# Batch 0's first transform stage on four 64x64 tiles, its input in pieces of 48 rows, its table and small inputs issued by ScalarE

## The chip, the cores and the metric

The kernel runs on one core of one Trainium2 chip. The metric is the device time of one execution in microseconds (us). The kernel before takes 1416.41 us, the median of three runs (1415.95 to 1417.36).

The engines are TensorE (PE for matmuls, PEld for weight loads), VectorE (DVE), ScalarE (ACT), GpSimd (POOL) and SyncE (SP), which here only issues DMAs. DMAs are issued in order on the queue of the engine that issues them.

## The reference

Two stages in float32. The first is a spectral layer on 4 batches of 3008 x 256, the second a mixture-of-experts style block with a rational activation on the 12032 resulting rows.

```python
X = np.fft.rfft(x, axis=1); Xr, Xi = X.real, X.imag
Yr = Xr @ w_r - Xi @ w_i + b_r
Yi = Xr @ w_i + Xi @ w_r + b_i
Yr, Yi = (np.sign(Y) * np.maximum(np.abs(Y) - 0.01, 0) for Y in (Yr, Yi))
y = np.fft.irfft(Yr + 1j * Yi, n=3008, axis=1).reshape(12032, 256)
h = y @ w_in                                    # 256 -> 2048
P = a[0] + a[1]*h + a[2]*h**2 + a[3]*h**3
Q = 1 + abs(b[0])*abs(h) + abs(b[1])*h**2
out = (P / (Q + 1e-6)) @ w_out                  # 2048 -> 256
```

## The kernel before

The transform of length 3008 = 64 x 47 is done as matmuls with tables. For each batch, stage f1 transforms along the 47 axis (rows padded to 48), its result goes out to a DRAM buffer `s1` and comes back with the axes turned (`b_all` for batch 0, `bt` for others); stage f2 transforms along the 64 axis; `m_task` mixes with w_r and w_i; `i1_task` is the first inverse stage, which goes out to `s2` and comes back as `ct`; `i2_task` is the last inverse stage and yields the input of the block, whose 208 units (L460, L553) are the main loop.

Batch 0's transform stands ahead of the main loop and is called the prologue here. It has these parts, in program order:

- Nine filler matmuls on a zero tile (`warm(9)`, L627), and eight loads of batch 0's input `x` on SP (`load_x`, L152). A load c holds four of the 32 columns j. Loads 0 and 1 have 96 rows of 4 KB, loads 2 to 7 have 128 rows, of which 96 are used.
- Stage f1 of batch 0 (`f1_first`, L173): 16 calls, two for each load c. A call is one float32 matmul of 96 rows by 128 columns of table `f1o` (a table with the two halves g interleaved) on 512 columns, then one copy out of PSUM, by ACT for the first call of a pair (L159) and by DVE for the second (L157). After a pair, SP stores 96 rows of 4 KB to `s1` (L187). Small steps that prepare bias and selection tiles (`prepare_small`) stand on DVE behind calls 9, 11, 13 and 15.
- On SP behind the stores: the first 8 of 24 pieces of table f2, the weights `wt`, the loads of `b_all` (L697, they need every store of `s1`), the rest of the tables, and the 16 raw loads of w_in and w_out, which come as float64 (L674).
- 33 filler matmuls (`warm(WARM)`, L729), then a loop over p of 12 pairs of frequencies: f2 (L255), mixing (L351, L358), i1 (L376). Between these stand the steps of the conversion of the raw weights to pairs of float32 tiles (`from_f64`, L597 to L611): five steps for each of 16 raw tiles, 80 in all. The numbers in `HC` and `HM` say how many steps stand at which p, `HF` how many behind the first five tasks of batch 1's stage f1.
- Batch 1's stage f1 (`f1_task`, L195), which runs on four tiles of 64x64: rows 0 to 47 and 64 to 111 hold the two halves g of the input, and each half is multiplied twice, for two pairs of columns.

All instructions stand on each engine in the order in which the program writes them. A DMA takes one of eight semaphores in turn (named DMAHW0 to DMAHW7 in the order), over both issuing engines, and an issue whose semaphore is still held by an earlier DMA waits for that one's landing.

Of the kernel before, what the change touches and what calls it, by code (L numbers as in the profile page):

```python
# [9 lines left out]
F32 = mybir.dt.float32  # L10
# [16 lines left out]
UB = NFC // FU  # L27
LAM = 0.01
WARM = 33
HC = (0, 0, 3, 3, 3, 3, 3, 3, 3, 3, 3, 3)  # L30
HM = (0, 0, 3, 4, 3, 4, 3, 4, 3, 4, 3, 4, 8, 0)
HF = (2, 3, 2, 0, 0)
I2Q = (5, 6)
SIZES = (5,) * 14 + (4,) + (5,) * 10 + (4,)
C0 = float(np.float32(1.0) + np.float32(1e-6))
# [2 lines left out]
def dft_tables():  # L38
    n2 = np.arange(N2)
    k2 = np.arange(NK)  # L40
    n1 = np.arange(N1)
    k1 = np.arange(N1)
    w = 2.0 * np.pi / N2
    ang = w * ((n2[:, None] * k2[None, :]) % N2)
    f1 = np.zeros((ROWS, NK, 2))
    f1[:N2, :, 0] = np.cos(ang)
    f1[:N2, :, 1] = -np.sin(ang)
    i2b = np.zeros((NK, NG, 2, NG, N2))
    i2 = np.zeros((NK, 2, N2))
# [24 lines left out]
    f1o = np.zeros((NG, ROWS, NK, 2, NG))
    for q in range(NG):
        f1o[q, :, :, :, q] = f1
    f1o = np.pad(f1o.reshape(96, 96), ((0, 0), (0, 32)))
# [12 lines left out]
    return {  # L90
        "f1": f1p.astype(f),
        "f1o": f1o.astype(f),
        "i2": i2p.astype(f),
        "f2": f2.reshape(128, NK * 128).astype(f),
        "g1": g.reshape(128, NK, 2, NG, NJ).swapaxes(2, 3).reshape(128, NK * 128).astype(f),
        "sel": sel.astype(f),
        "minus": -np.eye(128, dtype=f),
    }
# [3 lines left out]
def spectral_moe(ctx, tc, t, out):  # L102
# [39 lines left out]
    def load_x(b, c):  # L142
        if b == 1 and c in (2, 3):
            xt = pro3.tile([128, 4, D], F32, tag=f"x{c}", name="xin", bufs=1)
        elif b == 1 and c >= 6:
            xt = pro3.tile([128, 6, D], F32, tag=f"b{c - 6}", name="xin", bufs=1)[:, :4]
        elif b == 0 and c >= 2:
            xt = const.tile([128, 4, D], F32, tag=f"win{c}", name="xin")
        else:
            xt = sm.tile([128, 4, D], F32, tag="xin", name="xin")  # L150
        rows = 96 if b == 0 and c < 2 else 128
        nc.sync.dma_start(out=xt[:rows], in_=(t["x"][b - 1, c] if b else t["x0"][c])[:rows])  # L152
        xin[b, c] = xt

    def copy(eng, out, in_):
# [9 lines left out]
        while late:  # L165
            late.pop(0)()

    a_t = {}

    def new_s1(b):  # L170
        s1[b] = dram.tile([NK, 2, NG, NJ, D], F32, tag="s1", name="s1")

    def f1_first(i):  # L173
        c, r = divmod(i, 2)
        if i == 0:
            new_s1(0)
        pt = bank(0, "f1" if r else "")
        nc.tensor.matmul(out=pt, lhsT=f1o, rhs=xin[0, c][:96, 2 * r:2 * r + 2, :].rearrange("p j d -> p (j d)"),  # L178
                         start=True, stop=True)
        if not r:  # L180
            a_t[0] = const.tile([128, 4, D], F32, tag=f"wsp{c}", name="a")[:96]
        copy(r, a_t[0][:, 2 * r:2 * r + 2].rearrange("p j d -> p (j d)"), pt[:96])
        if r:
            del xin[0, c]
        if r or i >= 14:
            z = slice(2 * r, 2 * r + 2) if i >= 14 else slice(0, 4)
            nc.sync.dma_start(out=s1[0].rearrange("k c g j d -> (k c g) j d")[:, 4 * c + z.start:4 * c + z.stop, :], in_=a_t[0][:, z])  # L187

    def f1_task(b, c, pos):
        if pos == 0:  # L190
            new_s1(b)
        pts = [bank(b, "f1" if g else "m" if 4 <= pos < 6 else "") for g in range(NG)]
        for g, h in ((0, 0), (1, 1), (0, 1), (1, 0)):
            r = slice(64 * g, 64 * g + 48)
            nc.tensor.matmul(out=pts[g][64 * h:64 * h + 64], lhsT=f1[r],  # L195
                             rhs=xin[b, c][r, 2 * h:2 * h + 2, :].rearrange("p j d -> p (j d)"), start=True, stop=True)
# [415 lines left out]

    with tc.manual_schedule():
        nc.vector.memset(cb, 1.0)
        f1o = pro.tile([96, 128], F32, tag="f1o", name="f1o", bufs=1)
        nc.scalar.dma_start(out=f1o, in_=t["f1o"])
        nc.scalar.activation(out=cb, in_=cb, func=ACTF.Abs_reciprocal_sqrt)
        b_all = [pro3.tile([128, 6, D], F32, tag=f"b{z}", name="b_all", bufs=1) for z in range(4)]
        nc.vector.memset(offset, 0.0)
# [13 lines left out]
        eye = pro.tile([128, 128], F32, tag="eye", name="eye", bufs=1)  # L633

        def load_small():
            nc.sync.dma_start(out=sel, in_=t["sel"])
            for k, nm in enumerate(("b_r", "b_i")):
                nc.sync.dma_start(out=bsb[2 * k:2 * k + 2, :],
                                  in_=t[nm].rearrange("(o d) -> o d", o=1).to_broadcast([2, D]))
            nc.sync.dma_start(out=eye, in_=t["minus"])  # L640

        def prepare_small():
            nc.vector.memset(v32(selr), 0.0)
# [55 lines left out]
        def load_f2(a, z):  # L699
            nc.sync.dma_start(out=f2[:, a:z], in_=f2_src[:, a:z])  # L700
# [10 lines left out]

        load_small()
        small_steps = prepare_small()
        for i in range(16):
            f1_first(i)
            if i in (9, 11, 13, 15):
                next(small_steps, None)
        load_f2(0, 8)
        load_wt()
        prepare_mix()  # L720
        load_all(0, 2)
        load_all(2, 2)
# [8 lines left out]
        for p in range(np_ + 3):  # L731
# [11 lines left out]
            if p == 0:  # L743
                more_raw(2)
            elif p == 1:
                load_all(12, 6)
            elif p == 2:
                load_f2(12, 24)
                nc.sync.dma_start(out=ca, in_=t["a"].rearrange("(o d) -> o d", o=1).to_broadcast([128, 4]))
                nc.sync.dma_start(out=cb, in_=t["b"].rearrange("(o d) -> o d", o=1).to_broadcast([128, 2]))  # L750
                nc.sync.dma_start(out=i2, in_=t["i2"])
                nc.sync.dma_start(out=f1, in_=t["f1"])
            if p >= 1:
                more_raw(2)
            if p == 3:
# [188 lines left out]
```

## Time and profile before

| | us |
|---|---|
| median of three runs | 1416.41 |
| the profiled execution's own time | 1419.05 |
| its span, first to last instruction | 1417.3 |
| fillers and stage f1 of batch 0 end on PE | 21.7 |
| first matmul of f2 | 29.65 |
| first matmul of the main loop | 102.66 |

Times in the rows are counted from the span's start. The columns of the timeline are start, duration, engine, line, operation, output <- inputs, count of merged instructions, and in brackets the idle time before and what ended it. A float32 matmul shows as two records. The DMA share is the mean share of the 16 DMA engines' time that their packets took; where packets overlap it passes 100%.

### The profile page before, as it was taken

The page shows a single profiled execution, that of the slowest core. Times are in us where ns is not written, and L with a number is a line of the kernel's source. Part 1 is how long each engine was busy: PE and PEld are TensorE (multiplying, and loading weights), DVE is VectorE, ACT ScalarE, POOL GpSimd, SP SyncE. Part 2 cuts the span into 40 slices and gives each one's busy share as a digit, 9 for nine tenths or more (in the row PEclk, how much of TensorE's full clock was granted, in tenths as well). Part 3 has the DMA queues.
Part 4 walks back from the last instruction along what each step waited for, and adds up shares of the span by engine and source line. Part 5 has one row for each costly group of instructions (what it writes and reads, how often), then busy time and mean ns, then how long its engine had stood idle before and what let it go on. Part 6 is the DMA issues. An engine that isn't in the chain of part 4 may idle for free.

```text
span 1417.3 us, 20378 instructions
## 1 busy us (share of the span) xinstructions
PE 1390.0 (98%) x7279; PEld 1210.9 (85%) x7279; DVE 1291.5 (91%) x1304; ACT 1144.5 (81%) x1513; POOL 670.5 (47%) x444
## 2 busy tenths in 40 slices
PE   9998999999999999999999999999999999999997
PEld 4977889998878989898888899998888888888887
DVE  3779899898999989999989999999999999999998
ACT  2768887887888778888888778888888898888985
POOL 0444444444554444454545444444545555555553
PEclk9999999999999999999999999999999999999999
DMA  9966556556776556556687465656555465555543
GB/s 309 379 215 162 117 121 150 110 114 158 160 204 151 116 130 141 117 121 156 148 208 158 98 142 126 127 115 133 108 127 118 97 122 96 112 118 99 117 77 80
DMA packets 95657, 200.48 MB, mean 141 GB/s; under 512 B 10748, under 2 KB 51748, under 8 KB 95556
## 3 DMA queue, kind: packets, MB, share of 16 engines
q0 software_dynamic: 29664, 97.62, 38.0%
q1 hardware_dynamic: 65780, 101.51, 23.2%
q8 instruction: 58, 0.95, 0.3%
q14 instruction: 43, 0.35, 0.1%
q10 hardware_dynamic: 112, 0.05, 0.0%
HBM read 54.61 MB, written 37.49 MB: 65 GB/s over the span
## 4 chain that ended last, share of the span: by engine, by line
PE 72%; DVE 10%; issue 9%; ACT 5%; DMA 4%; SPq 0%; DVEq 0%; ACTq 0%
PE h L460 28%; PE acc L553 27%; PE pi L426 4%; PE pft L315 4%; DVE t L511 3%; DVE v L523 3%; PE pft L376 2%; DMA v<-s 2%; PE pft L297 2%; PE pft L255 2%; PE pft L195 1%; PE pft L178 1%; DVE g L520 1%; ACT t L499 1%; DMA s<-zt 1%
## 5 line engine op out<-in xcount | busy, mean ns | idle before, releaser
L553 PE MATMUL acc<-g,wsp 128*128 128x470 f32 (+1 forms) x2496 | 563.7, 375 | 3.4 <-DVE g L533 3.4
L527 POOL TENSOR_TENSOR t<-t,v 128x940 f32<-128x940 f32 (+1 forms) x206 | 469.7, 2280 | 164.4 <-DVE v L523 143.8
L553 PEld LDWEIGHTS acc<-g,wsp 128*128 128x128 f32 x2496 | 470.0, 190 | 62.8 <-DVE g L533 5.0
L460 PE MATMUL h<-xsh,win 128*128 128x470 f32 (+1 forms) x1664 | 436.9, 384 | 6.0 <-DVE t L512 5.6
L497 POOL DMA_DIRECT2D v<-s x206 | 181.6, 882 | 489.7 <-issue 452.9
L460 PEld LDWEIGHTS h<-xsh,win 128*128 128x128 f32 x1664 | 304.8, 189 | 61.6 <-PE acc L553 9.8
L520 DVE SCALAR_TENSOR_TENSOR g<-t,small,y 128x940 fp32r<-128x940 f32 (+1 forms) x208 | 250.3, 1203 | 45.8 <-ACT y L506 42.6
L492 ACT ACTIVATE v<-h 128x940 f32<-128x940 f32 (+1 forms) x208 | 196.2, 943 | 95.4 <-PE h L460 92.1
L511 DVE TENSOR_TENSOR t<-t,h 128x940 f32<-128x940 f32 (+1 forms) x208 | 231.3, 1112 | 27.3 <-ACT t L499 25.6
L512 DVE SCALAR_TENSOR_TENSOR t<-t,small,h 128x940 f32<-128x940 f32 (+1 forms) x208 | 245.2, 1179 | 7.4
L533 DVE SCALAR_TENSOR_TENSOR g<-t,small,y 128x940 fp32r<-128x940 f32 (+1 forms) x208 | 244.2, 1174 | 0.1
L460 PE MATMUL h<-xsl,win 128*128 128x470 f32 (+1 forms) x832 | 241.4, 371 | 0.0
L523 DVE SCALAR_TENSOR_TENSOR v<-v,g 128x940 f32<-128x940 f32 (+1 forms) x208 | 231.8, 1114 | 0.1
L504 ACT ACTIVATE y<-v 128x940 f32<-128x940 f32 (+1 forms) x208 | 206.1, 991 | 21.4 <-DMA v<-s 21.4
L499 ACT ACTIVATE t<-h,small 128x940 f32<-128x940 f32 (+1 forms) x208 | 216.2, 1039 | 0.0
L506 ACT ACTIVATE y<-y 128x940 f32<-128x940 f32 (+1 forms) x208 | 205.1, 986 | 2.0
L493 ACT ACTIVATE s<-h 128x940 f32<-128x940 f32 (+1 forms) x208 | 195.7, 941 | 0.0
L460 PEld LDWEIGHTS h<-xsl,win 128*128 128x128 f32 x832 | 155.8, 188 | 20.1
L426 PEld LDWEIGHTS pi<-small,ct 96*128 96x128 f32 x516 | 65.2, 192 | 7.9 <-ACT s L493 3.6
L426 PE MATMUL pi<-small,ct 96*128 96x94 f32 (+1 forms) x516 | 66.2, 275 | 3.5 <-DVE x L268 2.9
L159 ACT ACTIVATE pft<-offset 128x256 f32<-128x256 f32 x36 | 14.1, 391 | 57.6 <-DVE yt L321 23.3
L255 PEld LDWEIGHTS pft<-f,bt 128*128 128x128 f32 x288 | 37.3, 191 | 4.9 <-DVE yt L321 1.9
(113 smaller groups left out, 1071.0 us busy)
## 6 DMA issues: line engine op xcount, KB each, us to landing
v<-s POOLq DMA_DIRECT2D x190, 470.0 KB, 4.7
xin<-in_x SPq DMA_DIRECT2D x30, 512.0 KB, 6.4
s<-zt SPq DMA_DIRECT2D x48, 256.0 KB, 3.5
out_t<-ob SPq DMA_DIRECT2D x48, 235.0 KB, 4.5
ct<-s SPq DMA_DIRECT2D x20, 480.0 KB, 5.6
bt<-s SPq DMA_DIRECT2D x36, 256.0 KB, 3.3
y<-yt SPq DMA_DIRECT2D x144, 64.0 KB, 2.3
s<-a SPq DMA_DIRECT2D x46, 192.0 KB, 5.1
```

The lines of the kernel that those rows point to most:

```text
L460: nc.tensor.matmul(out=h[:, i, :w], lhsT=l, rhs=r, start=k == 0, stop=k == len(halves) // FU - 1)
L492: nc.scalar.activation(out=d["v"], in_=h, func=ACTF.Abs, scale=rate["b0"])
L499: nc.scalar.activation(out=d["t"], in_=h, func=ACTF.Identity, scale=rate["a3"], bias=ca[:, 2:3])
L504: nc.scalar.activation(out=d["y"], in_=d["v"], func=ACTF.Square, bias=C0)
L506: nc.scalar.activation(out=d["y"], in_=d["y"], func=ACTF.Abs_reciprocal_sqrt)
L511: nc.vector.tensor_tensor(out=tt, in0=tt, in1=h, op=ALU.mult)
L512: nc.vector.scalar_tensor_tensor(out=tt, in0=tt, scalar=ca[:, 1:2], in1=h, op0=ALU.add, op1=ALU.mult)
L520: stt(out=hi, in0=tt, scalar=ca[:, 0:1], in1=y, op0=ALU.add, op1=ALU.mult)
L523: stt(out=v, in0=v, scalar=C0, in1=v32(hi), op0=ALU.add, op1=ALU.mult)
L527: nc.gpsimd.tensor_tensor(out=tt[:, :cut], in0=tt[:, :cut], in1=v[:, :cut], op=ALU.subtract)
L533: stt(out=lo, in0=tt, scalar=ca[:, 0:1], in1=y, op0=ALU.add, op1=ALU.mult)
L553: nc.tensor.matmul(out=acc[n][e][:, :w], lhsT=l, rhs=r, start=begun[n][e] == 1, stop=begun[n][e] == 3 * FU * UB)
```

## The change

- `f1_first` is called 8 times, once for each load, and does what `f1_task` does: four matmuls of 48 rows by 64 columns on 512 columns, one on each quarter of the array, into two PSUM banks, one copied by ACT and one by DVE, both 128 x 512. The matmuls are in a new helper, `f1_mm`, used by both. The stores become 16, each 48 rows of two pieces of 2 KB.
- Batch 0's input is laid out as the others' (halves at rows 0 and 64) and loaded in 16 DMAs of 48 rows. Loads of the other batches take 112 rows instead of 128.
- The table is the one of the other batches, `f1` (128 x 64), loaded first on ACT's queue; the table `f1o` and the later load of `f1` on SP are gone. The four small inputs (`sel`, two biases, `eye`) go from SP's to ACT's queue, behind the activation at L617.
- Only 4 pieces of table f2 are loaded ahead of `b_all`, the next 8 behind its first three loads. The conversion starts one p later: `HC` and `HM` are 0 at p = 2, `HM` is 4 in place of 3, 4 in turn from p = 3 on, and `HF` is (2, 3, 2, 1, 1).

```diff
-HC = (0, 0, 3, 3, 3, 3, 3, 3, 3, 3, 3, 3)
-HM = (0, 0, 3, 4, 3, 4, 3, 4, 3, 4, 3, 4, 8, 0)
-HF = (2, 3, 2, 0, 0)
+HC = (0, 0, 0, 3, 3, 3, 3, 3, 3, 3, 3, 3)
+HM = (0, 0, 0, 4, 4, 4, 4, 4, 4, 4, 4, 4, 8, 0)
+HF = (2, 3, 2, 1, 1)
...
+        if b:
+            nc.sync.dma_start(out=xt[:112], in_=t["x"][b, c, :112])
+        else:
+            for g in range(NG):
+                nc.sync.dma_start(out=xt[64 * g:64 * g + 48], in_=t["x"][0, c, 64 * g:64 * g + 48])
...
+    def f1_mm(b, c, pts):
+        for g, h in ((0, 0), (1, 1), (0, 1), (1, 0)):
+            r = slice(64 * g, 64 * g + 48)
+            nc.tensor.matmul(out=pts[g][64 * h:64 * h + 64], lhsT=f1[r],
+                             rhs=xin[b, c][r, 2 * h:2 * h + 2, :].rearrange("p j d -> p (j d)"), start=True, stop=True)
+    def f1_first(c):
+        pts = [bank(0, "f1" if g else "") for g in range(NG)]
+        f1_mm(0, c, pts)
+        whole = const.tile([128, NG, 2, D], F32, tag=f"wsp{c}", name="a")
+        for g in range(NG):
+            copy(g, whole[:, g].rearrange("p j d -> p (j d)"), pts[g])
+        for h in range(2):
+            nc.sync.dma_start(out=dst[:, :, 4 * c + 2 * h:4 * c + 2 * h + 2], in_=whole[64 * h:64 * h + 48])
...
-        nc.scalar.dma_start(out=f1o, in_=t["f1o"])
+        nc.scalar.dma_start(out=f1, in_=t["f1"])
...
-            nc.sync.dma_start(out=sel, in_=t["sel"])
+            nc.scalar.dma_start(out=sel, in_=t["sel"])
...
-        for i in range(16):
-            f1_first(i)
-            if i in (9, 11, 13, 15):
+        for c in range(8):
+            f1_first(c)
+            if c >= 4:
                 next(small_steps, None)
-        load_f2(0, 8)
+        load_f2(0, 4)
...
-        load_f2(8, 12)
+        load_f2(4, 12)
```

SP at the program's start, before; `xin` is batch 0's input and `s` the buffer `s1`:

```order
L152 DMA xin<-in_x 96x1024 x2
L152 DMA xin<-in_x 128x1024 x5
L152 DMA xin<-in_x 128x1024 [waits DMAHW0_49]
L636 DMA sel<-in_sel 4x258 [waits DMAHW1_49]
L638 DMA bsb<-in_b_r 2x256 [waits DMAHW2_49]
L638 DMA bsb<-in_b_i 2x256 [waits DMAHW3_49]
L640 DMA eye<-in_minus 128x128 [waits DMAHW4_49]
L187 DMA s_136<-a 96x1024 [waits DMAHW5_49,DVE_49,Activation_49]
```

The same place now:

```order
L150 DMA xin<-in_x 48x1024 x3
L150 DMA xin<-in_x 48x1024 [waits DMAHW0_49]
L150 DMA xin<-in_x 48x1024 [waits DMAHW1_49]
L150 DMA xin<-in_x 48x1024 [waits DMAHW2_49]
L150 DMA xin<-in_x 48x1024 [waits DMAHW3_49]
L150 DMA xin<-in_x 48x1024 [waits DMAHW4_49]
```

Three pieces are issued freely instead of seven loads; the fourth waits for DMAHW0, which the table's DMA on ACT holds, and the small inputs, now on ACT, hold DMAHW3 to 5 and 7.

ACT where the conversion starts, before; L273 copies f2's result of one p, L597 and L598 begin the conversion of a raw tile, L364 takes the mixing's result:

```order
L273 ACTIVATE x<-pft 128x4x128 x3
L597 ACTIVATE e<-raw_win_225 128x512
L598 ACTIVATE r<-raw_win_225 128x512
L364 ACTIVATE yt<-pm 128x512
L597 ACTIVATE e<-raw_win_227 128x512
L598 ACTIVATE r<-raw_win_227 128x512
L609 ACTIVATE win_352<-e 128x2x256
L273 ACTIVATE x<-pft 128x4x128
```

The same place now (L270 is L273 before, L594 is L597, L361 is L364):

```order
L270 ACTIVATE x<-pft 128x4x128 x3
L361 ACTIVATE yt<-pm 128x512
L270 ACTIVATE x<-pft 128x4x128
L594 ACTIVATE e<-raw_win_255 128x512
L595 ACTIVATE r<-raw_win_255 128x512
L361 ACTIVATE yt<-pm 128x512
L594 ACTIVATE e<-raw_win_257 128x512
```

The first raw tile's conversion stands behind one more L361 and one more L270.

DVE at the prologue's end, before; `a` are copies of batch 1's stage f1, L600, L602 and L604 are conversion steps, L437 belongs to the main loop's first input:

```order
L157 COPY zt<-pft 128x512
L157 COPY a<-pft 128x512
L604 ISA e<-e,r 128x1024
L157 COPY a<-pft 128x512
L600 TENSOR_SCALAR e<-e 128x512
L602 SCALAR_TENSOR_TENSOR e<-raw_wsp_554,e 128x512
L157 COPY a<-pft 128x512
L604 ISA e<-e,r 128x1024
L157 COPY a<-pft 128x512 x2
L437 TENSOR_TENSOR xsl<-pi_1114,xsh 128x470
```

The same place now (L599 is L602 before, L601 is L604, L597 is L600, L434 is L437):

```order
L155 COPY zt<-pft 128x512
L155 COPY a<-pft 128x512
L599 SCALAR_TENSOR_TENSOR e<-raw_wsp_571,e 128x512
L155 COPY a<-pft 128x512
L601 ISA e<-e,r 128x1024
L597 TENSOR_SCALAR e<-e 128x512
L155 COPY a<-pft 128x512
L599 SCALAR_TENSOR_TENSOR e<-raw_wsp_573,e 128x512
L155 COPY a<-pft 128x512
L601 ISA e<-e,r 128x1024
L155 COPY a<-pft 128x512
L434 TENSOR_TENSOR xsl<-pi_1143,xsh 128x470
```

One more conversion step stands between `zt` and the main loop's first input, and the last L601 stands one copy later.

## Rows read from the trace of the kernel before

**Rows 1.** The page: busy time, share of the span and instructions of each engine.
```profile
PE 1390.0 (98%) x7279; PEld 1210.9 (85%) x7279; DVE 1291.5 (91%) x1304; ACT 1144.5 (81%) x1513; POOL 670.5 (47%) x444
```

**Rows 2.** The chain that ended last, in order of time: start, duration, what.
```profile
0.74 4.83 DMA f1o<-in_f1o
5.61 16.09 PE pft L178 x32
22.44 2.66 DMA s<-a
27.61 9.59 DMA raw_win<-in_w_in
```

**Rows 3.** Stretches of the prologue: busy time per engine, PEclk, DMA share, GB/s.
```profile
5.60:21.50 15.90, 15.89 (x32) 6.88 (x33) 6.70 (x15) 4.93 (x9) 0.00 (x0) 1.00 0.94 345
21.50:29.60 8.10, 7.31 (x34) 3.13 (x32) 1.61 (x4) 0.80 (x2) 0.00 (x0) 1.00 0.95 309
29.60:93.50 63.90, 60.69 (x451) 56.73 (x451) 48.36 (x79) 44.47 (x83) 27.38 (x24) 1.00 0.90 320
```

**Rows 4.** Timeline of PE, 0 to 33 us.
```profile
1.23 4.02 PE L625 MATMUL pft<-offset 128*128 128x512 bf16 x9 [1.23 <-DVE offset L619]
5.61 16.08 PE L178 MATMUL pft<-xin,f1o 96*128 96x512 f32 x32 [0.36 <-DMA f1o<-in_f1o]
21.53 7.29 PE L625 MATMUL pft<-offset 128*128 128x512 bf16 x33
29.65 1.13 PE L255 MATMUL pft<-f,b_all 128*128 128x128 f32 x8 [0.84 <-ACT wrh L661]
```

**Rows 5.** Timeline of PE's weight loads, 5 to 11 us.
```profile
8.33 0.34 PEld L178 LDWEIGHTS pft<-xin,f1o 96*128 96x128 f32 x1 [0.52 <-issue]
9.18 0.34 PEld L178 LDWEIGHTS pft<-xin,f1o 96*128 96x128 f32 x1 [0.52 <-issue]
9.94 0.19 PEld L178 LDWEIGHTS pft<-xin,f1o 96*128 96x128 f32 x1 [0.42 <-issue]
```

**Rows 6.** Timeline of SP's issues, 0 to 30 us.
```profile
0.74 5.17 SPq L152 DMA_DIRECT2D xin<-in_x  x8
10.78 11.97 SPq L187 DMA_DIRECT2D s<-a  x9
25.17 1.40 SPq L697 DMA_DIRECT2D b_all<-s  x3
```

**Rows 7.** DMA: GB/s in 40 slices of 0 to 6 us.
```profile
GB/s 0 0 0 0 0 0 0 0 0 0 0 82 137 109 61 68 198 130 396 403 317 416 396 191 263 294 222 276 164 191 218 273 164 355 164 273 191 328 246 191
```

**Rows 8.** DMA of 6:11 (two rows), 11:16, 25.3:29.6, 100:112 and 106:108.
```profile
DMA packets 552, 2.01 MB, mean 401 GB/s; under 512 B 62, under 2 KB 62, under 8 KB 552
...
q1 hardware_dynamic: 552, 2.01, 102.1%
...
DMA packets 700, 2.02 MB, mean 404 GB/s; under 512 B 89, under 2 KB 225, under 8 KB 700
...
DMA packets 914, 1.54 MB, mean 358 GB/s; under 512 B 64, under 2 KB 694, under 8 KB 914
...
DMA packets 1701, 3.38 MB, mean 282 GB/s; under 512 B 288, under 2 KB 288, under 8 KB 1699
...
DMA packets 389, 0.73 MB, mean 366 GB/s; under 512 B 57, under 2 KB 57, under 8 KB 389
```

**Rows 9.** Timeline, 92 to 104 us: batch 1's stage f1 on four tiles, its DVE copy.
```profile
91.94 1.09 PE L195 MATMUL pft<-xin,small 48*64 48x512 f32 x8
93.39 0.68 DVE L157 COPY a<-pft 128x512 f32<-128x512 f32 x1
```

**Rows 10.** Timeline of ACT where the conversion starts.
```profile
37.22 0.66 ACT L597 ACTIVATE e<-raw_win 128x512 f32<-128x512 f32 x1 [3.38 <-DMA raw_win<-in_w_in]
```

**Rows 11.** Timeline of DVE and ACT at the prologue's end.
```profile
98.03 0.69 DVE L602 SCALAR_TENSOR_TENSOR e<-raw_wsp,e 128x512 uint32<-128x512 uint32 x1
99.24 1.16 DVE L604 CUSTOM_DVE_ANT_0 e<-e,r 128x1024 uint16<-128x1024 uint16 x1
100.43 0.63 ACT L609 ACTIVATE wsp<-e 128x512 fp32r<-128x512 f32 x1 [1.48 <-DVE e L604]
101.92 0.56 ACT L429 ACTIVATE xsh<-pi 128x470 fp32r<-128x470 f32 x1
```

More of the change, by code (lines that the diff above doesn't have):

```diff
@@ L73, in dft_tables @@
     g[1, :, :, 1] = cot * wi.T[:, :, None]
[L74 to L77, printed above, removed]
     f1p = np.zeros((NG, 64, 64))
@@ L91, in dft_tables @@
         "f1": f1p.astype(f),
-        "f1o": f1o.astype(f),
         "i2": i2p.astype(f),
@@ L150, in load_x @@
             xt = sm.tile([128, 4, D], F32, tag="xin", name="xin")
-        rows = 96 if b == 0 and c < 2 else 128
-        nc.sync.dma_start(out=xt[:rows], in_=(t["x"][b - 1, c] if b else t["x0"][c])[:rows])
+        if b:
[3 more added lines that the diff above has]
+                nc.sync.dma_start(out=xt[64 * g:64 * g + 48], in_=t["x"][0, c, 64 * g:64 * g + 48])
         xin[b, c] = xt
@@ L166, in flush @@
             late.pop(0)()
-    a_t = {}
     def new_s1(b):
         s1[b] = dram.tile([NK, 2, NG, NJ, D], F32, tag="s1", name="s1")
-    def f1_first(i):
-        c, r = divmod(i, 2)
-        if i == 0:
-            new_s1(0)
[L177 to L187, printed above, removed]
+    def f1_mm(b, c, pts):
[4 more added lines that the diff above has]
+    def f1_first(c):
+        if c == 0:
+            new_s1(0)
+        pts = [bank(0, "f1" if g else "") for g in range(NG)]
[3 more added lines that the diff above has]
+            copy(g, whole[:, g].rearrange("p j d -> p (j d)"), pts[g])
+        del xin[0, c]
+        dst = s1[0].rearrange("k c g j d -> (k c) g j d")
+        for h in range(2):
+            nc.sync.dma_start(out=dst[:, :, 4 * c + 2 * h:4 * c + 2 * h + 2], in_=whole[64 * h:64 * h + 48])
     def f1_task(b, c, pos):
@@ L192, in f1_task @@
         pts = [bank(b, "f1" if g else "m" if 4 <= pos < 6 else "") for g in range(NG)]
[L193 to L196, printed above, removed]
+        f1_mm(b, c, pts)
         yield
@@ L614, in spectral_moe @@
         nc.vector.memset(cb, 1.0)
-        f1o = pro.tile([96, 128], F32, tag="f1o", name="f1o", bufs=1)
-        nc.scalar.dma_start(out=f1o, in_=t["f1o"])
+        nc.scalar.dma_start(out=f1, in_=t["f1"])
         nc.scalar.activation(out=cb, in_=cb, func=ACTF.Abs_reciprocal_sqrt)
@@ L635, in load_small @@
         def load_small():
-            nc.sync.dma_start(out=sel, in_=t["sel"])
+            nc.scalar.dma_start(out=sel, in_=t["sel"])
             for k, nm in enumerate(("b_r", "b_i")):
-                nc.sync.dma_start(out=bsb[2 * k:2 * k + 2, :],
+                nc.scalar.dma_start(out=bsb[2 * k:2 * k + 2, :],
                                   in_=t[nm].rearrange("(o d) -> o d", o=1).to_broadcast([2, D]))
-            nc.sync.dma_start(out=eye, in_=t["minus"])
+            nc.scalar.dma_start(out=eye, in_=t["minus"])
         def prepare_small():
@@ L751, in spectral_moe @@
                 nc.sync.dma_start(out=i2, in_=t["i2"])
-                nc.sync.dma_start(out=f1, in_=t["f1"])
             if p >= 1:
@@ L924 @@
     for g in range(NG):
-        xg = x.reshape(B, N2, NG, NJ // 4, 4, D)[:, :, g].swapaxes(1, 2)
-        xp[0, :, g * ROWS:g * ROWS + N2] = xg[0]
-        xp[1:, :, g * 64:g * 64 + N2] = xg[1:]
-    arrays = {"x": xp[1:], "x0": xp[0], **dft_tables()}
+        xp[:, :, g * 64:g * 64 + N2] = x.reshape(B, N2, NG, NJ // 4, 4, D)[:, :, g].swapaxes(1, 2)
+    arrays = {"x": xp, **dft_tables()}
     w = np.stack([inputs[n] for n in ("w_r", "w_i")])
```

## The prediction

> **What bounds the kernel now.** I read the page first: PE is busy 98% of the span [rows 1], so what happens late hides nothing and is worth what PE loses. The change touches batch 0's first stage, so I read the chain of waits next, at its start. It runs through that stage without a break [rows 2]: table `f1o` lands at 5.57 us, PE works on L178 until 21.7, a DVE copy follows, the last store is issued at 22.44 and lands 2.66 later, at 25.10. The loads of `b_all` come behind it [rows 6], and f2 starts at 29.65 [rows 4]. The windows by stage [rows 3] show what is full in each stretch: PE from 5.6 to 21.5 (15.89 of 15.90 us); the DMA engines at a share of 0.94 and 0.95 up to 29.6; then PE again, 60.69 of 63.90 us up to 93.5. So an earlier f2 brings the rest of the prologue forward, if the DMAs, at 0.90 on average over that stretch, come forward too. Nothing in the main loop changes but the size of its input loads, so a gain there should reach the end undiminished.
>
> **Stage f1.** Before, 32 records take 16.08 us [rows 4], in two paces: weight loads take 0.34 us up to 9.18 and 0.19 from 9.94 [rows 5], and their starts are 0.85 and 0.43 apart. [...] Now one load costs what four tiles cost: batch 1's take 1.09 us for eight records, at full clock [rows 9], of which I count 0.9 as pace and the rest as overlap. Eight loads take 7 to 9 us in place of 16, or about 14 at half clock throughout (8 x 1.72, twice the pace of 0.86 that 2 x 0.43 gives). PE thus stops being the bound of this stage; the copies, 0.68 each on DVE [rows 9], are no longer than the matmuls. The small preparing steps now stand between closer copies, but all of DVE's work from 5.6 to 29.6 is 8.3 us [rows 3], which ends by about 16 even if it is done in one piece behind the first load. The DMAs come next.
>
> **Input.** 16 pieces of 48 x 4 KB are 3.15 MB; before it was 960 rows, 3.93 MB. The engines moved 401 to 404 GB/s at a share of 102% [rows 8], so by bytes alone 0.79 MB are worth 2.0 us. Against this stands a stall. Only three pieces (0.59 MB) can be issued before the fourth waits for the table, which landed 4.83 after its issue at 0.74 [rows 2]. Now it is 32 KB instead of 48 and has less beside it: between 2.7 (the last store's landing time) and 4.83, I take 4.1, so 4.8 us. First bytes moved about 1.0 us after the first issue (slice 12 of 0.15 us against 0.74) [rows 7, 6]. The transfers resume at 5.8, with the three pieces done. The other 2.56 MB at 402 GB/s take 6.4 us: the input is through at 12.2. (Issues are no limit: eight loads took 5.17 us with one wait among them [rows 6].)
>
> With the engines full, I price the input by bytes and give the split itself nothing. [...]
>
> **Stores.** They are 3.15 MB as before, but in pieces of 2 KB. At 404 GB/s (a window with stores of 4 KB among loads) they take 7.8 us; at 282 GB/s (batch 1's stores of 2 KB and less, with pauses) 11.2; I take 366, the window that holds batch 1's stores alone with full engines [rows 8]: 8.6. PE and the copies follow the input by about two to four microseconds and their last store is issued by 16 to 18, before the engines could start on it. So the stores are through at 12.2 + 8.6 = 20.8, and land at 21.9: of the last store's 2.66 us, about 1.0 is the start and 0.5 its own 192 KB, which leaves 1.1 behind the last byte. Against 25.10, 3.2 us are won (0.6 to 4.0 by the two ends).
>
> **f2's start.** Before, from the last landing to the first matmul it took 4.5 us [rows 2, 4], since 1 MB of f2 and `wt` had been issued just ahead of the loads. Now 0.79 MB stand there, directly behind the stores: 2.2 us at 358 GB/s [rows 8] from 20.8, to 23.0, then 0.7 for the first 256 KB and 1.1 to land: 24.8. The old 4.5 from 21.9 gives 26.4; a bare landing of 2.7 gives 24.6. I take 25.1, so 4.5 us are won here. The DMA stream behind it is as long as before, and starts as much earlier as the stores end, plus a little for what was idle: I take 4.2 for it, and the smaller of the two holds from here on: **-4.2**.
>
> **The conversion.** Before, ACT waits 3.38 us for the first raw tile at 37.22 [rows 10] with the mixing's result queued behind it. Now the conversion stands one p later, about 4.9 us in PE's time (63.9 over 13). The raw tile comes 4.2 sooner, at 33.0; ACT arrives there at about 33.3. So nothing is queued behind a late DMA and the step costs nothing; the cover is ACT's own work for p = 3. If the raw tiles were 2 us later, ACT would wait 1.7, and PE's next i1, five microseconds off, would still be covered. From p = 3 on there are seven steps at each p in place of six and a half. PE's idle time, 3.2 us in this stretch [rows 3], could go either way by one: zero, with plus and minus 1.
>
> **The end of the prologue.** The steps that are put off come back here. One L602 (0.69 us) more stands on DVE between `zt` and the first input of the main loop, and the last L604 stands one copy later. Before, ACT's L609 waited for that L604 until 100.43, with one more copy and L429 at 101.92 behind it [rows 11], and PE's second half waits for L429. DVE has about a microsecond free earlier in the stretch, and one ACT copy moves ahead of L609. Bounds 0 and 1.4 (step and copy in full); I take half: **+0.7**.
>
> The remaining edits cost nothing on the path: the small inputs leave SP, where they stood between waits, and ACT has no copy to do before the table lands; 112 rows for 128 save DMA time under PE-bound work.
>
> **Sum.** -4.2 + 0.7 = -3.5. The profiled execution takes 1419.05 us with a span of 1417.3, so it becomes 1415.5 with a span of 1413.8. The runs' median stands 2.6 below the profiled execution: 1416.41 - 3.5 = 1412.9. A change of 0.2% (2.8 us) is about what a measurement can tell from none.
>
> **Rivals.**
>
> *PE stays at half clock through the stage and the fillers: slower.* The four-tile work comes in bursts, one per piece of input. For it: a gap of 0.36 in the fillers was followed by four more microseconds at half clock [rows 4, 5]. Against it: half-clock work for a load (1.72 us) is longer than the input's pace of one per microsecond, so PE is soon busy without gaps. If it stays, the loads are through at 7.4 + 7 x 1.72 = 19.4, and 33 fillers at 0.43 (double of 7.29 / 33) take 14.2: f2 starts at 33.6, 4 us late, and the time is 1421. It decides once the fillers end past 25; if the clock rises in mid-fillers, as four microseconds in full columns did, f2 starts near 28.7 and the result is no change.
>
> *PE waits for `b_all` and its clock drops.* The 33 fillers end at about 15.5 + 7.3 = 22.8 and f2 comes at 25.1: a gap of 2.3 us, where it was 0.84 [rows 4]. If the clock fell, 4 to 8.7 us (the climb at the program's start, from 1.23 to 9.9) would run at half rate and lose 2 to 4.3: 1415 to 1417, no change. No row shows such a gap. [...]
>
> *The DMAs give less.* Stores at 282 GB/s end at 23.4, land at 24.5, and f2 starts at 27.5: 2.1 won, 0.7 lost, 1415.0, no change. The same if each piece's wait for its semaphore leaves the engines idle.
>
> *The DMAs give more.* Stores at 404 GB/s, the table at 3.5 and a free end: -5.8, 1410.6.
>
> **Chances.** Forecast 48% (1411.5 to 1414.5), half clock throughout 8%, clock drop 12%, slower DMAs 18%, more 14%. Faster by over 0.2%, below 1413.6: the 14%, four fifths of the forecast and a few points of the third and fourth: 57%. Within: 34%. Slower: most of the first rival and a little of mishandled steps in the conversion, 9%. The range leaves out the half-clock rival and the far end of the fast one: 1409.6 to 1417.2.
>
> **What would show it.** The fourth input piece issued at 4.8 and DMA empty around 5; input through near 12; stage f1 over by 15 to 18 with PE waiting for input, stores at a steady rate and the last landing at 22; f2 at 25.1; ACT's first L594 without a wait over 1 us; i2 3.5 us sooner and the main loop's L460 at 99.2. Wrong would be: f2 before 23.5 or after 27.5, fillers at 0.43, PE idle by more than 4.5 us between f2 and 93, or a main loop that is not the same length from its first L460 on.

## The result: 8 us slower, and the profile after

The changed kernel takes 1424.86 us, the median of six runs (1423.44 to 1426.51), against 1416.88 (1415.93 to 1418.2) for the kernel before on the same chip: a ratio of 1.0057, with a 95% interval of 1.0044 to 1.007. Forecast were 1412.9 us; the time lies above the range. The profiled execution of after takes 1424.84 us with a span of 1423.1, that of before 1419.05 with 1417.3. "Lag" below is by how much an instruction starts later than the same one in before's profiled execution.

The page of after; PE's busy time is within 0.3 us of [rows 1], so the loss is not more work:

```profile
PE 1390.3 (98%) x7311; PEld 1207.8 (85%) x7311; DVE 1293.7 (91%) x1304; ACT 1145.7 (81%) x1513; POOL 670.7 (47%) x444
```

The chain of waits of after (start, duration, what), which answers to [rows 2]. There it ran through PE's work on stage f1; now it runs through the input's DMAs from 6 to 19.4 us, through SP's issues of the stores up to 25.5 (not among the lines shown), and through DMAs again up to 33.8:

```profile
0.74 3.60 DMA small<-in_f
6.11 5.51 DMA xin<-in_x
11.64 7.76 DMA xin<-in_x
25.57 3.46 DMA s<-a
29.17 4.59 DMA b_all<-s
```

The table lands at 4.34, as early as forecast. Then the DMA totals of after for 6 to 18 us, which is the input, and for 19 to 23 us, when stores alone run:

```profile
DMA packets 786, 2.39 MB, mean 200 GB/s; under 512 B 197, under 2 KB 197, under 8 KB 786
...
q1 hardware_dynamic: 786, 2.39, 103.9%
...
DMA packets 899, 1.59 MB, mean 396 GB/s; under 512 B 132, under 2 KB 132, under 8 KB 898
```

From 6 to 18 us the engines are full (a share of 1.04), as at 401 GB/s in [rows 8] (1.02), and move half as much. SP's queue moves 0.76 MB before 6 us and 2.39 up to 18, together the 3.15 of the input: its last packets start at about 18.0 and take 0.34 us each, so it is through at about 18.4, not 12.2. PE waits for it, as its timeline shows (compare [rows 4]):

```profile
5.18 15.44 PE L173 MATMUL pft<-xin,small 48*64 48x512 f32 x64
20.55 7.30 PE L621 MATMUL pft<-offset 128*128 128x512 bf16 x33
33.90 2.05 PE L252 MATMUL pft<-f,b_all 128*128 128x128 f32 x8 [6.05 <-DMA b_all<-s]
36.59 1.63 PE L252 MATMUL pft<-f,b_all 128*128 128x128 f32 x8
38.27 1.05 PE L252 MATMUL pft<-f,b_all 128*128 128x128 f32 x8
```

A load's eight records come every 2 us. The fillers end at 27.85, f2 comes at 33.90 instead of 29.65, and its first eight records take 2.05 us where they took 1.13. SP's issues (compare [rows 6]) and the windows by stage (busy time per engine, PEclk, DMA share, GB/s; compare [rows 3]):

```profile
0.74 11.21 SPq L150 DMA_DIRECT2D xin<-in_x  x16
12.72 13.59 SPq L187 DMA_DIRECT2D s<-a  x16
29.17 1.41 SPq L693 DMA_DIRECT2D b_all<-s  x3
```

```profile
26.00:28.00 2.00, 1.85 (x9) 0.65 (x7) 0.00 (x0) 0.00 (x0) 0.00 (x0) 1.00 0.84 246
33.90:35.70 1.80, 1.80 (x8) 1.77 (x9) 0.11 (x1) 0.00 (x0) 0.00 (x0) 0.50 0.81 292
33.90:98.10 64.20, 62.86 (x451) 58.42 (x451) 46.24 (x70) 43.19 (x80) 27.25 (x24) 0.97 0.91 306
```

The second row shows the granted clock at 0.50 of full behind the wait of 6.05 us. From the lag of 4.25 us at f2's start it goes to 6.1 at the third p, falls to 4.6 at 67 us and stands at 4.72 where batch 1's f1 begins. Then comes the prologue's end (timeline of after; compare [rows 11]):

```profile
99.90 1.13 PE L373 MATMUL pft<-yt,g 128*128 128x256 f32 x4 [1.50 <-DVE yt L364]
...
105.49 1.77 DVE L599 SCALAR_TENSOR_TENSOR e<-raw_wsp,e 128x512 uint32<-128x512 uint32 x1
...
108.49 0.63 ACT L606 ACTIVATE wsp<-e 128x512 fp32r<-128x512 f32 x1 [2.16 <-DVE e L601]
...
110.11 2.00 PE L457 MATMUL h<-xsh,win 128*128 128x470 f32 x8 [0.96 <-ACT xsh L426]
```

The last row started at 102.66 before: a lag of 7.45. At the end it is 5.8; before's profiled execution stood 2.2 above its median, and the medians differ by 8.0. What the lag loses in the main loop, 1.65, is that execution's and not the change's: in two kernels below that differ from before in the tables alone it falls by 1.93 and 1.74 there. In the same two, f2 starts at 27.89 and at 29.53 behind an unchanged program, so a lead or a lag of f2 below 2 us says nothing by itself.

### The profile page after: what moved, and what is told of

Its sections match the earlier page's. It is cut to its first block, busy times and chain, and to the rows that moved or that the text cites. A ratio compares the mean times of both kernels' runs of the same rounds, so it can differ in the third digit from the quotient of the medians.

```text
span 1423.1 us, 20461 instructions
## 1 busy us (share of the span) xinstructions
PE 1390.3 (98%) x7311; PEld 1207.8 (85%) x7311; DVE 1293.7 (91%) x1304; ACT 1145.7 (81%) x1513; POOL 670.7 (47%) x444
## 4 chain that ended last, share of the span: by engine, by line
PE 72%; DVE 11%; issue 9%; ACT 4%; DMA 3%; SPq 1%; DVEq 0%; ACTq 0%; POOLq 0%
PE h L457 28%; PE acc L550 27%; PE pft L312 4%; PE pi L423 4%; DVE t L508 3%; DVE v L520 3%; PE pft L252 3%; PE pft L373 3%; PE pft L294 2%; PE pm L355 2%; DMA xin<-in_x 1%; PE pft L173 1%; DVE g L517 1%; DMA v<-s 1%; ACT t L496 1%
## 5 line engine op out<-in xcount | busy, mean ns | idle before, releaser
L173 PE MATMUL pft<-xin,small 48*64 48x512 f32 x248 | 41.9, 627 | 0.2
```

## The experiments

### Who pays for the pieces: whole rows, and pieces in the kernel before

After with batch 0's input in eight loads of 128 rows; and the kernel before with each of its loads in two halves of 48 rows.

```diff
 after:  -for g in range(NG): dma_start(out=xt[64 * g:64 * g + 48], ...)
         +dma_start(out=xt, in_=t["x"][0, c])
 before: +for g in range(NG): dma_start(out=xt[48 * g:48 * g + 48], ...)
```

> The changed kernel, with batch 0's input loaded as eight DMAs of 128 rows instead of sixteen of 48; all else as changed. In the changed kernel the input moved at 197 to 209 GB/s with full engines, against 401 before. If the pieces are the cause (by rows, by source block or by number), the input goes back to about 400 GB/s: 4.19 MB are through near 13, the last store lands near 23, f2 starts near 26.5 instead of 33.9 and the time falls by 7 to 9 us, to 1416 to 1418. If instead ScalarE's small DMAs or the lower number of free issues slow the input, the rate stays near 200 and the time near 1425.

> The kernel before, with each of batch 0's eight loads split into two of 48 rows (rows 0 to 47, 48 to 95); nothing else. If the pieces alone make the input slow, the input moves at about 200 GB/s, is through near 17 to 18, stage f1 on PE ends near 24 instead of 21.7, and the time rises by 2 to 5 us. If they do so only together with the four tiles or ScalarE's queue, the rate stays near 400 and the time within 1 us of before.

Whole rows in after: 1422.65 (1421.75 to 1424.63), ratio 1.0044 [1.0032, 1.0056]. Stage f1 ends at 17.4, but only 2.2 us are won: the stores behind it go at 242 and 235 GB/s, and f2 starts at 30.61 after a wait of 5.96, its first eight records taking 2.05 us. Halves in before: 1421.78 (1421.12 to 1422.37), ratio 1.0035 [1.0022, 1.0047]; f2 at 33.73. So the pieces alone make a kernel slow, without tiles or tables. The halves' DMA total for 6 to 11 us:

```profile
DMA packets 362, 1.11 MB, mean 222 GB/s; under 512 B 91, under 2 KB 91, under 8 KB 362
```

### What makes a piece slow

Five kernels, a change in the loads alone: after with the two halves of a row side by side in DRAM, so that the rows of a piece lie 8 KB apart instead of 4; the kernel before with each half on every second of 96 partitions; after with 16 pieces of 128 rows and 2 KB; and the kernel before cut in 64 + 32 and in 32 + 64 rows.

```diff
 dramstep: in_=t["x0"][c, :, g]                                # [48, 2, 1024]
 every2:   out=xt[g:96:2]
 columns:  out=xt[:, 2 * h:2 * h + 2]
 sides:    for r in (slice(0, 64), slice(64, 96)): dma_start(out=xt[r], ...)
 cross:    for r in (slice(0, 32), slice(32, 96)): dma_start(out=xt[r], ...)
```

> The changed kernel, with the input in DRAM laid out so that the rows of a piece lie 8 KB apart instead of 4 KB (both halves of a row side by side); destinations, pieces and order unchanged. If the source's closeness (one block of 192 KB read by 16 engines) makes the pieces slow, a packet of 4 KB falls from 340 ns to near 160 and the rate rises to near 400 GB/s. If the 48 destination rows do, both stay at about 200 GB/s.

> The kernel before, with each of batch 0's loads split into two of 48 rows, each written to every second of 96 partitions (the table's rows are permuted to match). In b_halves, with 48 neighbouring partitions, packets of 4 KB took about 305 ns and the input moved at 211 to 231 GB/s. If a transfer is slow because its rows lie on few neighbouring partitions, it is faster here: 300 to 400 GB/s, PE's stage f1 starts its pairs sooner and f2 starts 2 to 4 us before that of b_halves (33.7). If it is slow because a transfer has only 48 rows or 192 KB, rate and f2's start are those of b_halves.

> The changed kernel with batch 0's input in sixteen pieces that are each 128 rows of 2 KB (half of a row's columns) instead of 48 rows of 4 KB. If the number of DMAs or their size made the input slow (sixteen instead of eight, 192 KB each): 190 to 250 GB/s as in the changed kernel, stage f1 ending after 20 us. If the 48 neighbouring partitions did it: 350 to 400 GB/s from 6 to 14 us, the stage ending at about 17 us as with whole rows (17.4), f2's first matmul near 30.6 us and a time near 1422.

> The kernel before with each of batch 0's loads (96 rows of 4 KB) in two pieces: rows 0 to 63 and rows 64 to 95. [...] Rival Q (what counts is the number of rows or of transfers): 64 and 32 rows, 350 and 200 GB/s, or about 290, and the same in both kernels of this pair.

> The same with the cut elsewhere: rows 0 to 31 and rows 32 to 95, again one piece of 32 and one of 64 rows. [...] Rival Q: as with the cut at row 64.

Times: 1426.26, 1422.21, 1423.63, 1424.05, 1417.24, one run each; only the rates are read from them. DMA totals for 6 to 11 us (of the columns 12 to 16, since from 6 to 12 the share was only 0.79 to 0.91), in this order:

```profile
DMA packets 315, 0.98 MB, mean 195 GB/s; under 512 B 77, under 2 KB 77, under 8 KB 315
```
```profile
DMA packets 464, 1.43 MB, mean 286 GB/s; under 512 B 115, under 2 KB 115, under 8 KB 464
```
```profile
DMA packets 871, 1.59 MB, mean 397 GB/s; under 512 B 96, under 2 KB 96, under 8 KB 871
```
```profile
DMA packets 384, 1.18 MB, mean 236 GB/s; under 512 B 96, under 2 KB 96, under 8 KB 384
```
```profile
DMA packets 466, 1.46 MB, mean 293 GB/s; under 512 B 109, under 2 KB 109, under 8 KB 466
```

Neither the source's layout (195 GB/s with the rows 8 KB apart) nor the number of DMAs nor their size (397 with 16 of 128 rows) is the cause. The last two kernels have the same pieces of 64 and 32 rows and differ only in the partitions that a piece reaches, and in the rate by a quarter (236 and 293 GB/s), against rival Q. So the partitions count. By rate:

| batch 0's load, partitions of the pieces | GB/s, measured |
|---|---|
| 0-47, 64-111 (after) | 200 |
| 0-47, 48-95 | 222 |
| 0-63, 64-95 | 236 |
| every second of 96 | 286 |
| 0-31, 32-95 | 293 |
| 128 rows | 397 to 417 |

Pieces of 0-47 and 64-111 in turn ran at 206 GB/s from 6 to 11 us in after. What makes one set of partitions faster than another is not shown. Which partitions a piece reaches was not weighed in the prediction.

### Is it enough to hide the wait for `b_all`: more fillers

> The changed kernel with 58 fillers ahead of f2 instead of 33, so that PE works from 20.6 to about 33.4 and does not wait 6.05 us for b_all. If PE's clock fell in that wait, the first eight records of f2 take 1.1 us instead of 2.05, the third f2 starts about 1.9 us sooner, and the time falls by 1 to 2 us, to 1423 to 1424. If the slow f2 has another cause (late tables), nothing moves.

After with `WARM = 58`: 1425.97 (1425.19 to 1428.29), ratio 1.0069 [1.0054, 1.0083].

```profile
34.51 1.13 PE L252 MATMUL pft<-f,b_all 128*128 128x128 f32 x8 [0.37 <-DMA b_all<-s]
...
38.37 1.13 PE L252 MATMUL pft<-f,b_all 128*128 128x128 f32 x8 [1.19 <-DMA f<-in_f]
```

The clock stays up (f2's first eight records take 1.13 us for 2.05, behind a wait of 0.37 us for 6.05), so its fall does come from the wait. The time doesn't follow: the third f2 waits for the part of table f2 that the change put behind `b_all`. What PE gains at f2 it loses in that wait.

### The conversion tables

Three kernels: before with after's `HC`, `HM`, `HF`; after with before's; before with the first steps moved to p = 3 and two steps at `HM`'s p = 12 (10 for 8) in place of `HF`'s two.

> The kernel before with the new HC, HM and HF alone. In the changed kernel PE's lag fell by 1.5 us between p = 3 and p = 8 and rose by 2.7 between the last p and the first matmul of the main loop. If both come from the new places of the conversion, the lag here is about -1.5 at p = 8, +1 at the main loop's start, and the time rises by 0.5 to 2 us. If the end's loss comes from DMAs that land late, the time does not rise: 1415 to 1417.

> The changed kernel with the conversion tables HC, HM and HF of the kernel before. Theory (of the 8 us that the changed kernel loses, the tables give back about 1.3 us by the middle of the prologue and cost about 2.7 at its end): f2 starts 4 to 4.5 us late as in the changed kernel, the lag rises to 6 or more at p=2 and, with the wait for raw_win there again, stays at 5.5 to 6.5 to the first h (7.46 in the changed kernel), a time of 1423 to 1425, 0 to 1.5 under the changed kernel. Rival (the prologue's end loses 2.7 us in any kernel whose f2 starts late, by the same order of transfers): the lag still rises by over 2 us between 92 and 110 us, a time of 1425 to 1427.

> The kernel before with the conversion's first steps moved from p=2 to p=3 and later, as in the changed kernel's HC and HM, but with its own HF (two steps more at HM's p=12 instead). If the moved first steps win 0.8 to 1.3 us by p=4 and the two extra steps in HF cost the 2.7 us at the prologue's end: lag -1 to -1.3 at the first h and a time 0.5 to 1.5 us under the kernel before (ratio 0.9990 to 0.9996). If the steps at p=12 cost the same as in HF (they stand in front of the first batch 1 copies on ScalarE): lag 0 to +1.5 and a time of 0 to 2 us over it.

Tables in before: 1419.23 (1416.91 to 1423.05), ratio 1.0018 [1.0005, 1.003]. Its lag is -1.76 at f2 (stage f1 was done in 14.0 us), -2.81 at batch 1's f1, -0.07 at the first h: 1.05 won in the loop, 2.74 lost at its end, in the same two places as in after:

```profile
92.37 1.13 PE L376 MATMUL pft<-yt,g 128*128 128x256 f32 x4 [1.49 <-DVE yt L367]
...
102.58 2.01 PE L460 MATMUL h<-xsh,win 128*128 128x470 f32 x8 [0.96 <-ACT xsh L429]
```

In both kernels DVE's step ahead of the second place (L602 here, L599 in after) takes 1.77 us instead of 0.68, which is as much as is lost there; no run separates the two.

Old tables in after: 1422.53 (1421.18 to 1425.16), ratio 1.0043 [1.0028, 1.0058]; its lag falls from 7.88 behind the third p to 6.24 at 67 us and stays there to the first h, without a step at the end. So the end's loss is the tables', but the fall in the loop is not: with the old tables it is 1.64, with the new ones 1.38 (up to batch 1's f1), at the same two i1, where PE of before had waited 0.50 and 1.11 us. With an f2 that comes late those waits are gone whatever the tables.

The third kernel: 1417.5 (1415.12 to 1424.24), ratio 1.0014 [1.0002, 1.0025], lag 0.48 at batch 1's f1 and 2.14 at the first h, above both ranges of the expectation. Two more steps at p = 12 cost 1.66, all at the first of the two places; the second, and its 1.1 us, belongs to `HF`.

### Four tiles without the slow loads

After with whole loads, before's tables, 128-row loads throughout, small inputs on SP and 45 fillers; the same with every second store issued by ACT; and with `s1` laid out so that a store's row is one piece of 4 KB.

```diff
 four:  load_x whole, HC/HM/HF of before, load_f2(0, 8), WARM = 45
 split: +(nc.scalar if h else nc.sync).dma_start(... whole[64 * h:64 * h + 48])
 wide:  s1 [NK, 2, NG, NJ, D] -> [NK, 2, NJ // 2, NG, 2, D]
```

> The changed kernel with what the earlier runs found slow undone: batch 0's input in eight loads of 128 rows, the small inputs on SP behind them, HC, HM, HF, the split of f2 and the 128 rows of the other batches as before; 45 fillers for 33. What is left is the four tiles, their stores in sixteen DMAs, and table f1 for f1o. If the stores move at full rate once the input is through (404 GB/s), the last lands at 21 to 22 and f2 starts at 25 to 26: the time is 1412 to 1414. If SyncE's issue of the stores (0.55 us and more each, in place of 0.30) or their pieces of 2 KB hold them back, the last lands near 25 and f2 starts near 29 to 30: 1416 to 1418.

> c_four with every second store issued by ScalarE instead of SyncE. If the issue on one queue holds the stores back, the last lands 1 to 3 us sooner than in c_four and the time falls by as much. If the transfers themselves do (pieces of 2 KB from 48 rows), nothing is won, or ScalarE's copies are held up by its own waits and 0 to 2 us are lost.

> The kernel of the run before last (four tiles, whole 128-row loads, the tables and small inputs of the kernel before), with the scratch tensor s1 laid out so that each row of a store is one piece of 4 KB instead of two of 2 KB; the table f2 has its rows in the matching order. Theory A (the sixteen stores are held back by their issue: 0.55 to 0.9 us of SP for each with 96 pieces of 2 KB, against 0.30 in the kernel before with 96 pieces of 4 KB; the packets, 110 to 120 ns each against 84 to 86 where a queue of stores had built up, are slow because too few are in flight): issues of about 0.3 us, 350 to 400 GB/s between 14 and 21 us, b_all issued at 22 to 23 us (26.73 there), f2's first matmul at 26.5 to 28 us (31.49 there), a time of 1419 to 1423. Theory B (stores run at about 250 GB/s whatever their pieces, as the kernel before also shows 236 to 288 GB/s from 18 to 24 us): the issues may be shorter, but 14 to 26 us stay at 230 to 270 GB/s and b_all is issued at 26 to 27 us, a time of 1426 to 1427. Theory C (48 neighbouring partitions are the cause, as with the loads): as B, with packets of 4 KB at over 200 ns.

1426.82, 1426.57 and 1424.58 us (ratios 1.0068 [1.0051, 1.0085], 1.005 [1.0034, 1.0066], 1.0049 [1.003, 1.0068]). The input now runs at 403 to 417 GB/s and stage f1 ends at 15.2, but f2 starts at 31.49 in the first: the stores take until 26.7. A second issuing engine doesn't change that (28.5, f2 at 32.72), but it is no clean test, as ACT's copies wait behind its issues (PE waits 2.84 us for one of them) and stage f1 ends at 18.5. The larger pieces test it cleanly: the first issues come down to 0.30 us, and the stores still run at 283 and 230 GB/s from 14 to 22 us, until 26.0, with f2 at 30.40. So theory A falls; B and C are left. Windows of the first:

```profile
14.00:18.00 4.00, 3.83 (x20) 1.59 (x22) 3.21 (x9) 1.39 (x3) 0.00 (x0) 1.00 0.86 241
18.00:22.00 4.00, 4.00 (x20) 1.86 (x19) 0.00 (x0) 0.00 (x0) 0.00 (x0) 1.00 0.86 250
```

### Stores on all partitions

The first of these with one DMA for all 128 rows of a result (padding too), and `s1` read in two DMAs of 64 rows; then the same with 60 fillers.

```diff
-for h in range(2): dma_start(out=dst[:, :, 4*c+2*h:4*c+2*h+2], in_=whole[64*h:64*h+48])
+dma_start(out=s1[0][:, c], in_=whole)
```

> The kernel with four tiles, whole loads of batch 0, the old tables and 45 fillers (c_four), with the scratch tensor laid out so that one DMA stores all 128 partitions of a load's result, 4 KB each (the rows of padding go with them: 512 KB for 384), and each reading of it in two DMAs of 64 partitions. [...]

> The kernel that stores all 128 partitions with one DMA (t_two), with 60 fillers instead of 45, so that TensorE works until b_all lands near 28.6 us. Theory (the clock's fall after the wait of 3.56 us costs what it did there, from -0.95 us at f2's first matmul to +1.97 at the fourth): f2's first eight matmuls 1.1 us instead of 2.05, lag -0.9 to -0.2 up to 40 us. From there two readings of 64 rows per tile instead of one cost the 1 us that they cost in t_two (+1.97 to +2.91 by 92 us) and the prologue's end the 1.6: +0.3 to +1.5 at the first h, a time of 1418 to 1420, 2.5 to 4 under t_two and not under the kernel before. Rival (the clock's fall costs nothing that waits for transfers would not cost anyway): the lag at 40 us is +1.5 or more again, a time of 1421.5 to 1423.

```profile
14.00:18.00 4.00, 3.72 (x20) 1.53 (x22) 3.15 (x9) 1.39 (x3) 0.00 (x0) 1.00 1.02 416
18.00:22.00 4.00, 4.00 (x21) 1.81 (x19) 0.00 (x0) 0.00 (x0) 0.00 (x0) 1.00 1.03 417
```

So the stores' pace hangs on the partitions too (theory C): 416 GB/s instead of 241. These stores are also half as many and larger; the columns kernel excludes that as a cause for loads, no run does for stores. f2 starts at 28.70, 0.95 before the profiled execution of before and 0.8 behind the 27.89 of the tables kernel. The time is 1422.15 (1421.92 to 1423.28), ratio 1.0037 [1.0023, 1.0051]: behind a wait of 3.56 us f2's first eight records take 2.05 us (lag +1.97 by the fourth). With 60 fillers it is 1424.02 (1420.91 to 1429.7), ratio 1.0056 [1.0038, 1.0075]:

```profile
28.84 1.13 PE L251 MATMUL pft<-f,b_all 128*128 128x128 f32 x8 [0.63 <-ACT wih L656]
...
37.26 1.13 PE L251 MATMUL pft<-f,b_all 128*128 128x128 f32 x8 [1.59 <-DMA b_all<-s]
```

The lag is -0.8 for three p and +1.1 at the fourth, which waits for its part of `b_all`, and 4.69 at the first h. The theory is wrong and the rival nearer, though the time lies above both ranges: without the clock's fall (1.13 us for f2's first eight records) as much time goes in waits for transfers. But these two kernels are no test of four tiles with every transfer at full rate. Their stores move a third more bytes, and each reading of `s1` goes in two DMAs of 64 rows; that this makes them slow is likely and not shown. DMA totals for 25 to 30 us, when `b_all` is read, of before and of the first:

```profile
DMA packets 1046, 1.73 MB, mean 346 GB/s; under 512 B 72, under 2 KB 793, under 8 KB 1046
...
DMA packets 878, 1.12 MB, mean 225 GB/s; under 512 B 101, under 2 KB 771, under 8 KB 878
```

### What was left at the prologue's end

With old tables, 4 KB pieces and 68 fillers; later batches' loads of 112 or of 128 rows.

> The kernel with four tiles, whole 128-row loads of batch 0, stores in pieces of 4 KB and the conversion tables of the kernel before (c_four_wide), now with 68 fillers instead of 45, so that TensorE works until b_all lands near 30.3 us, and with the changed kernel's 112-row loads for the later batches. Theory (the losses are the pieces, the clock and the tables, and nothing else): f2's first eight matmuls 1.1 us instead of 2.04, lag at f2 about +0.8 and at p=2 +0.8 to +1.2 instead of +2.66, 0 to -0.8 from 67 to 98 us, no stretch at half clock at 104 us, the same or -0.8 at the first h, a time of 1415 to 1417.5. Rival (the prologue's end loses its 3 to 6 us whenever stage f1 is in four tiles): lag back to +3 or more at 106 us, a time of 1419 to 1424.

> The same with 128-row loads for the later batches, as in the kernel before. If these loads delayed the store of zt and the load of ct at 97 to 102 us in c_four (4.6 us from the store's issue to the load's, 2.5 us in the kernel before) and so brought the stretch at half clock: the lag rises by 2 to 5 us between 98 and 110 us here and not with 112 rows, a time 2 to 5 us longer than with 112. If not, the two agree within 1 us.

1420.93 (1419.56 to 1423.07), ratio 1.0032 [1.0019, 1.0044], and 1421.36 (1417.35 to 1424.78), ratio 1.0034 [1.0022, 1.0047]: the rows don't matter. The second differs from the kernel with pieces of 4 KB in its fillers alone, 68 for 45, and f2 starts at 30.40 in both. First and third p of f2, with 45 and with 68 fillers:

```profile
30.40 2.04 PE L251 MATMUL pft<-f,b_all 128*128 128x128 f32 x8 [5.51 <-DMA b_all<-s]
34.82 1.05 PE L251 MATMUL pft<-f,b_all 128*128 128x128 f32 x8
...
30.40 1.13 PE L251 MATMUL pft<-f,b_all 128*128 128x128 f32 x8 [0.49 <-DMA b_all<-s]
32.91 1.05 PE L251 MATMUL pft<-f,b_all 128*128 128x128 f32 x8
```

So here the fillers win 1.91 us by the third p, and no later wait takes it back: the lag from 67 to 98 us is -0.88 instead of 1.0. All that is lost comes behind it: 2.7 at the first h, 5.2 at 142. Timeline of PE, and the DMA queues for 90 to 95 us:

```profile
101.07 4.66 PE L422 MATMUL pi<-small,ct 96*128 96x94 f32 x20 [1.50 <-ACT a L156]
105.37 3.22 PE L456 MATMUL h<-xsh,win 128*128 128x470 f32 x8
```

```profile
q1 hardware_dynamic: 544, 0.52, 31.8%
q8 instruction: 1, 0.02, 2.2%
```

An instruction fetch of 16 KB, one packet on one DMA engine, lies on the store of `zt` that the main loop's first input hangs on; the store lands 4.4 us after its issue (2.4 in the kernel with after's tables in before, where no such packet lies there). PE waits 1.5 us and then works at half clock (0.50 of full granted from 102 to 106 us): 4.66 us for what takes 2.52 in before. A like stretch is in c_four (0.50 granted from 104 to 112 us, 4.66 us), in its variant with pieces of 4 KB (4.34) and in the 112-row kernel (4.66); after and a_tables don't have it (2.52 in both). No run moved the fetch alone, but it falls elsewhere in each kernel. The 20 traces have 40 gaps from the issue of a store of `zt` to the issue of the load of `ct` that waits for it: with a 16 KB fetch running, 3.05 to 4.64 us (8 gaps); without one, 2.14 to 2.51 (30 gaps) and twice more (3.04 and 3.51), each just behind a late one and a load of 256 KB. So fetch and delay go together; that a filler or a tile moves the fetch there is not shown.

## Why the prediction was wrong

| step | forecast | measured |
|---|---|---|
| table lands | 4.8 | 4.34 |
| input through | 12.2 | 18.4 |
| last store lands | 21.9 | 29.03 |
| f2 starts | 25.1 | 33.90 |
| change until batch 1's f1 | -4.2 | +4.7 |
| prologue's end | +0.7 | +2.75 |
| sum | -3.5 | +7.45 at the main loop's start; medians +8.0 |

- **The step that failed is Input**: "I price the input by bytes and give the split itself nothing." [Rows 8] gave 401 GB/s for loads of 128 rows; no row showed a load of 48. The pieces ran at 200 GB/s with the engines as full, and the input was through 6.2 us later than forecast. No rival had a slow input in it: "the DMAs give less" lowers the stores alone. The halves kernel shows it without the rest of the change. A full share was read as a full rate: 1.02 went with 401 GB/s in before, 1.04 with 200 in after.
- **Stores** were mis-sized too: 366 GB/s came from a window of the main loop, while the same stage of before shows 239 from 18 to 22 us. In after a queue of stores runs at 396 GB/s from 19 to 23 and at 246 later, on average near the forecast, so this cost little here. It is what keeps whole loads from helping: 2.2 us won of the 6.
- **f2's start** follows from both. "Issues are no limit" was right for the input, which kept the engines at a share of 1.04.
- **The rival with the clock drop came true** on top (0.50 of full after 6.05 us of waiting, +1.85 us), from a wait that I had put at 2.3. What it is worth depends on what comes next: with 58 fillers in after and with 60 in the kernel with 64-row reads the time went in a later DMA wait; with 68 in the kernel where no later transfer was late, 1.91 us were won back. Fillers alone could not have saved the forecast: f2's lag of 4.25 stays.
- **PE at half clock through the stage**, the rival that ended slower, did not happen: the clock is granted in full from 7 to 30 us, and the fillers take 7.30. (Its own price is a little low: 33 fillers at double of 7.29 / 33 take 14.6, not 14.2.) That the engine was at half clock up to 9.2 us in before was read from the weight loads of [rows 5]; the PEclk of 1.00 that [rows 3] give for 5.6 to 21.5 doesn't show it. In the columns kernel the rival's half clock did come about: a granted clock of 0.50 from 14 to 18 us, behind a wait of 1.18 for input.
- **The conversion**: PE won 1.38 over the loop in after, just above "zero, plus and minus 1", but behind an f2 that late the old tables won as much (1.64). In the two kernels with the new loop tables and before's loads it was 1.05 and 1.04.
- **The prologue's end** was bounded at 1.4 and cost 2.75. ACT's wait ahead of L606 was foreseen (it cost about 1.1, and goes with the slow L599); the wait of PE for `yt`, 1.50 for 0.50, with a slower set of eight matmuls ahead (1.74 for 1.09), was not: 1.65.

So the change exchanged PE time that had run beside DMAs for DMA time on the path. No kernel here with four tiles beat the one before. Whether one could stays open: none had loads, stores and reads of `s1` all at full rate, and the one that was level with before up to 98 us lost most of its time behind the late store at the prologue's end.

## What to carry to other kernels

A DMA share of 1.0 is no rate (1.04 went with 200 GB/s here): before a transfer is cut or moved to other partitions, look for a row with that very shape, and count how many partitions it reaches and which (pieces of 64 and 32 rows: 236 or 293 GB/s). When PE is made faster in a stage, add up the bytes of that stage first: here whole loads brought the end of stage f1 to 17.4 us but the time fell by only 2.2, as the stores behind it went at 242 and 235 GB/s. Count in it what the new layout does to the reads behind. And here a wait that was made longer cost its length and then the clock (6.05 us, then 0.50 of full), while filling it helped only where the next transfer wasn't late as well (1.91 us won with 68 fillers; with 58 and 60 the next waits were 1.19 and 1.59 us). Before a lag against one profiled execution is read, look where that execution stands among its kernel's runs.

## What the runs showed of the hardware

- Loads of 48 rows, partitions 0 to 47 and 64 to 111 in turn: about 200 GB/s at a DMA share of 1.04; every second of 96: 286; 32 to 95 with 0 to 31: 293; 128: up to 417 at 1.03. Stores of 48 rows of a half: 241 and 250 GB/s from 14 to 22 us in c_four, where they come one by one, and 396 in after where a queue of them had built up; 128 rows: 416.
- DVE's L599 took 1.77 us instead of 0.68 where GpSimd's L608 started 0.05 us before it; in the kernel with after's tables in before, L602 took 1.77 with L611 0.05 ahead.
- A 16 KB instruction fetch beside a store of 256 KB: the load that waits for the store is issued 3.05 to 4.64 us after it, in 8 gaps; 2.14 to 2.51 in 30 of the 32 without a fetch.
